# A gated MLP beside a state-space scan: Up weights in three blocks, the skip row's vector behind the B transposes, two table rows ahead of a table load, stacked half products last

## The chip, the cores and the metric

The kernel runs on one core of one Trainium2 chip. The core has a matrix engine (PE, with its weight loads shown as PEld), a vector engine (DVE), an activation engine (ACT), a general engine (POOL) and a sync engine whose queue (SP) issues most of the DMAs. The metric is device time in microseconds of one execution; less is better. The engines run side by side and meet only at semaphores.

## The reference

The input x has 2,048 tokens of 448 features. After a layer norm without weights, two branches read the normalised tokens, and their product is added to x:

```python
x = A_x
xn = _layernorm(x, axis=-1)
s = _A_ref(xn, ...)                      # diagonal complex state space, scan over the tokens
g = _silu(_B_ref(xn, B_w_gate, B_w_up, B_w_down))
return x + s * g
```

Branch A projects xn to 448 complex states by B (its real and imaginary matrices), runs `h = Lam_bar * h + Bu[t]` over all tokens, projects back by C and adds `xn * Dskip`, the skip row. Branch B is a gated MLP: `(sigmoid(xn @ w_gate) * (xn @ w_up)) @ w_down` with 1,792 hidden features. All inputs and the output are bf16.

## The kernel before

The tokens are cut into four chunks of 512 (four tiles of 128 each). For a chunk the kernel needs xn with the features on the partitions (`xnT`). Chunk 0 gets it by PE transposes, chunks 1 to 3 by DMA transposes that SP issues (`dma_transpose`, through the helper `tload`, L394).

**Gate and Up.** The 1,792 hidden features are seven steps m of 2 x 128. One step (`gu_mm`, L809 and L810) is seven pairs of matmuls with 64 contraction rows each: L809 uses partitions 0 to 63 of the weight tile and L810 partitions 64 to 127, at the same time, into the two halves of one PSUM buffer `gu` (there are three; for the fourth Gate step of chunk 0 the two `acc` banks are used). A Gate step is emptied by ACT (a tanh, L843 or L840), an Up step by DVE (L846), which multiplies the two. In chunk 0 all seven Gate steps run first, then all seven Up steps.

**Weights.** `load_w` loads one block of steps of one half (64 partitions) with one DMA on SP; the table `BLK` says which steps form a block. Gate has the blocks (0, 2), (2, 4), (4, 7), Up has (0, 3), (3, 7); each block is two DMAs, one for each half. One DMA has 64 x 7 rows of 256 bytes for each step of its block (two steps: rows of 512 bytes).

**B phase.** `b_phase` projects a chunk's xn by B into the states. B has 448 rows of features, and 448 is 3 x 128 + 64, so beside three full contraction blocks (`fulls`, L897 and L900) there is a half block (`halfrows`): L883 for the state groups 0, 1 and 2, and L886 for group 3, where the real and imaginary part are stacked on the partitions (from the tile `bT6`). Four groups of half products open or close the accumulation; the function `pairs` issues those of groups 3, 0 and 1 in this order as the first matmuls of the phase. The B matrices come by DMA transposes on SP (`b_load`): `bT` blocks 0 to 2 and block 3 of each matrix. From them POOL copies the stacked tile `bT6` (L748, L754), and DVE copies the half block of the real matrix from the upper to the lower 64 partitions (L751, key `bT3l`).

**Tables.** The scan works in a rotating frame and needs cosines and sines for 513 positions and four state groups. `scale` (L668, ACT) multiplies the positions by a group's angle, `tables` rounds on DVE (L677, L679) and takes the sines on ACT. The angle `turn` is made by POOL (L656, L658). ACT needs the silu table set for its tanh, sine and silu (`silu_table`, L664), and a set for square roots before it.

**Skip row.** `skip_row` (L545, DVE) multiplies xn by Dskip, which a DMA spreads over all partitions into the tile `dbc`.

**The order of the work.** Every operation is registered with `add` in a plan: its engine, a cost, what it reads and writes. PE's operations, and the DMAs marked `chain`, keep the order in which they are registered on their engine; so do DVE's and ACT's while `pl.seq` is true. All others are placed by a list scheduler (`solve`) by due times that follow from PE's order, from the costs, and from the times in `land`, at which a DMA is assumed to land. `HEAD_DMA` is the number of first DMAs that the scheduler numbers by registration when it models that at most eight DMAs are out at once. None of these times is a wait in the kernel: they only set the order in which each engine gets its instructions.

**The end.** `yout` makes an output tile: PE multiplies by C (L1044), DVE adds the skip row, multiplies by the gate and adds x (L1066 to L1068), SP stores it (L1057). For chunk 2 the stores of tiles 1, 2 and 3 are cut into two halves of 64 rows.

Lines of the profile that the prediction uses besides: L450 statistics of a tile of x (DVE), L540 widening copy of xn (POOL), L981 last write of the states hT of a group (DVE), L1025 the Down matmuls.

Of the kernel before, what the change touches and what calls it, by code (L numbers as in the profile page):

```python
# [18 lines left out]
D = 448  # L19
F = 1792  # L20
P = 128
H = 64
# [4 lines left out]
TPC = L // P  # L27
NTAB = L + 1
EPS = 1e-5
HEAD_DMA = 17  # L30
TWO_PI = 2.0 * math.pi
PI = math.pi
MAGIC = 12582912.0
# [213 lines left out]
def kernel(  # L247
# [18 lines left out]
    V, A, G, T, Q = nc.vector, nc.scalar, nc.gpsimd, nc.tensor, nc.sync  # L266
# [84 lines left out]
    add = pl.add  # L351
# [9 lines left out]
        load(q, [("x", t) for t in range(t0, t0 + n)], n * P * D * 2,  # L361
             x_all[:, t0:t0 + n, :], x_src[:, t0:t0 + n, :], r=r, rate=rate, land=land)

    BLK = {"g": [(0, 2), (2, 4), (4, 7)], "u": [(0, 3), (3, 7)]}

    def load_w(eng, k, half, b, r=(), rate=105e3, land=0.0):
        m0, m1 = BLK[k][b]
# [63 lines left out]
    add("POOL", 0.15, lambda: G.memset(flat(g_raw[:, 512:2048], 3, 512)[:, :, D:512], 0.0),  # L431
        w=[("xnw", t) for t in (1, 2, 3)])
    load_w("SP", "u", 0, 0, rate=400e3, land=15.6)
    load_w("SP", "u", 1, 0, rate=400e3, land=17.3)
    load_x(6, 2, land=19.3)
    load_w("SP", "u", 0, 1, rate=400e3, land=20.9)
    load_w("SP", "u", 1, 1, rate=400e3, land=22.5)
    load("SP", "dbc", P * D * 2, dbc[:], A_Dskip.unsqueeze(0).to_broadcast((P, D)), rate=400e3, land=22.7)


    def warm_mm(n, w=512):
# [224 lines left out]
    def scale(pt):  # L666
        turn, v = C("turn"), v_t[:, pt, :]
        add("ACT", 0.61, lambda: A.activation(v, iota[:, 0:NTAB], ACT.Copy, scale=turn[:, pt:pt + 1]),  # L668
            r=[("wv", 0), "turn", "silutab"], w=[("v", pt)])

    def tables():
        for pt in range(4):
            vk, nk = ("v", pt), ("nu", pt)
            v, nu = v_t[:, pt, :], nu_t[:, pt, :]
            if pt:
                scale(pt)
            add("DVE", 0.4, lambda v=v, nu=nu: V.tensor_single_scalar(out=nu, in_=v, scalar=MAGIC, op=ALU.add),  # L677
                r=[vk], w=[nk])
            add("DVE", 0.6, lambda v=v, nu=nu: V.scalar_tensor_tensor(out=nu, in0=nu, scalar=-MAGIC, in1=v,  # L679
                                                                      op0=ALU.add, op1=ALU.subtract),  # L680
                r=[vk, nk], w=[nk])
            add("ACT", 0.5, lambda v=v, nu=nu: A.activation(v, nu, ACT.Abs), r=[nk, "silutab"], w=[vk])
            so, co = (spm[:, pt, 0, :], cosT[:, pt, :]) if pt < 3 else (cs3[:, 1, :], cs3[:, 0, :])
            add("ACT", 0.537, lambda so=so, nu=nu: A.activation(so, nu[:, 0:L], ACT.Sin, scale=-S),
                r=[nk, "silutab"], w=[("sin", pt)])
            add("ACT", 0.624, lambda co=co, v=v: A.activation(co, v[:, 0:L], ACT.Sin, scale=-S, bias=pio2[:]),
                r=[vk, "silutab", "pio2"], w=[("cos", pt)])
            if pt < 3:
                add("DVE", 0.2, lambda pt=pt: V.tensor_single_scalar(out=spm[:, pt, 1, :], in_=spm[:, pt, 0, :],
                                                                     scalar=-1.0, op=ALU.mult),  # L690
                    r=[("sin", pt)], w=[("nsin", pt)])
        vs, ns = [("v", p) for p in range(4)], [("nu", p) for p in range(4)]
        cth, sth = C("cth"), C("sth")
        add("ACT", 0.2, lambda: A.activation(sinL[:, :, 0, :], nu_t[:, :, L:L + 1], ACT.Sin, scale=-S),
            r=ns + ["silutab"], w=["sinL"])
        add("ACT", 0.2, lambda: A.activation(cosL[:], v_t[:, :, L:L + 1], ACT.Sin, scale=-S, bias=pio2[:]),
            r=vs + ["silutab", "pio2"], w=["cosL"])
        add("ACT", 0.2, lambda: A.activation(sth[:].unsqueeze(2), nu_t[:, :, 1:2], ACT.Sin, scale=-S),
            r=ns + ["silutab"], w=["sth"])
        add("ACT", 0.2, lambda: A.activation(cth[:].unsqueeze(2), v_t[:, :, 1:2], ACT.Sin, scale=-S, bias=pio2[:]),  # L700
            r=vs + ["silutab", "pio2"], w=["cth"])
        add("POOL", 0.3, lambda: G.tensor_single_scalar(out=sinL[:, :, 1, :], in_=sinL[:, :, 0, :], scalar=-1.0,
                                                        op=ALU.mult), r=["sinL"], w=["nsinL"])

        gate([("vrow", q) for q in range(3)], [("hF", 0, m) for m in range(7)])
# [37 lines left out]

    def b_load():
        for i, m in enumerate((A_B_re, A_B_im)):
            tload([("bT", i)], bT[:, 0:3, i, :], m[:, 0:384], D * 768, land=24.0 + 1.4 * i)
            tload([("bT3", i)], bT[:, 3:4, i, :], m[:, 320:448], D * 256, land=24.4 + 1.8 * i)
            add("POOL", 0.7, lambda i=i: G.tensor_copy(out=bT6[:, 0:3, i * H:i * H + H], in_=bT[:, 0:3, i, 384:448]),  # L748
                r=[("bT", i)], w=[("bT6", i)])
            if i == 0:  # L750
                add("DVE", 0.3, lambda: V.tensor_copy(out=bT[0:H, 3, 0, :], in_=bT[H:P, 3, 0, :]),  # L751
                    r=[("bT3", 0)], w=["bT3l"])
            for h in range(2):
                add("POOL", 0.25, lambda i=i, h=h: G.tensor_copy(out=bT6[h * H:h * H + H, 3, i * H:i * H + H],  # L754
                                                                        in_=bT[H:P, 3, i, 384:448]),
                    r=[("bT3", i)], w=[("bT6", i, h)])
# [115 lines left out]
    def b_phase(c, mid=None):  # L872
# [14 lines left out]
                             start=start, stop=not start)  # L887

        def pairs():
            for pt in (3, 0, 1):  # L890
                halfrows(pt, True)

        def fulls(pt, first):
# [166 lines left out]
    def yout(c, j, first=False):  # L1060
        t = c * TPC + j
        g, o, q = gt_of[c, j], next_o(), t % NXD
        a = next_acc()
        key, ok, od = ("acc", a), ("o", o, 0), o_t[o][:]
        y = y_mm(c, j, acc[a], key, 0, D, False, first)
        add("DVE", dve1(D), lambda: V.tensor_tensor(out=od, in0=y, in1=xd[q][:], op=ALU.add), r=[key, ("xd", q)], w=[ok])  # L1066
        add("DVE", dve2(D), lambda: V.tensor_tensor(out=od, in0=od, in1=g_t[g][:], op=ALU.mult), r=[ok, ("gt", g)], w=[ok])
        add("DVE", dve2(D), lambda: V.tensor_tensor(out=od, in0=od, in1=x_all[:, t, :], op=ALU.add), r=[ok, ("x", t)], w=[ok])  # L1068
        rows = (0, H, P) if c == 2 and j else (0, P)
        for r0, r1 in zip(rows, rows[1:]):  # L1070
            store(t, od, 0, D, r0, r1, [ok])

# [68 lines left out]
    for t in (1, 2, 3):  # L1141
        shift(t, 1, "DVE")
        shift(t, 0, "DVE")
    gate(uk, ("gu", u2))
    silu_table()
    scale(0)
    pl.seq = False
    for t in (1, 2, 3):
        last_tile(0, "g", steps01, t, ("c", 1, "b"))
    for m in range(2):  # L1150
        gu_evac(0, "g", m, slots0[m])
    gu_mm(0, "g", 2, slots0[2], 0, TPC, False)
    gu_evac(0, "g", 2, slots0[2])
    gu_mm(0, "g", 3, None, 0, TPC, False)
    gu_evac(0, "g", 3, None)
    b_load()
    def stats_for(c):
        for t in range(4 * c, 4 * c + 4):
            if c not in (3,):
                stats(t)  # L1160
            elif t % 2:
                act_stats(t - 1)
            if t % 2:
                chain(t - 1, 2)
# [97 lines left out]
```

## Time and profile before

| what | value |
|---|---|
| median of 3 runs | 183.93 us (183.44 to 184.11) |
| the profiled execution's own time | 183.8 us |
| its span in the trace | 182.0 us |
| busy, PE | 176.8 us |
| busy, DVE | 165.9 us |
| busy, ACT | 98.1 us |
| busy, POOL | 35.1 us |
| DMA: bytes moved | 13.43 MB |
| granted clock of PE, mean | 0.997 |

How to read it: the span is the time from the first to the last recorded instruction of the profiled execution, and its own time is what the same execution was measured at; what lies between them (1.8 us) is outside the trace. Times in rows are microseconds from the span's start unless marked ns. A row of a timeline is start, duration, engine, line, operation, output <- inputs, partitions x elements, and in brackets the idle time before it with what ended it. A row of a window is the stretch, its length, and for each engine its busy time with the number of instructions; the last three numbers are PE's granted clock, the mean busy share of the 16 DMA engines and the GB/s they moved. A matmul's row shows 0.38 us for 512 columns, but the next one starts 0.21 us after it, because they are pipelined: on PE it is the starts that count.

### The profile page before, as it was taken

To read this page: it belongs to the slowest core of one execution; us is meant where nothing else is said; L and a number is where in the kernel's file an instruction comes from. 1 tells how busy PE (TensorE), PEld (TensorE's weight loads), DVE (VectorE), ACT (ScalarE), POOL (GpSimd) and SP (SyncE) were. 2 spreads that over 40 slices of the span, in tenths; PEclk is the share of its full clock that TensorE was granted. 3 is DMA by queue.
4 is the path that set the end of the run, shared out by engine and by line. 5 is a ranking of instruction groups with operands and counts; after the bars stand their busy time and mean duration, and the time that the engine had idled before them with its cause. 6 is when DMAs were issued, how large, how long until landed. Compare 5 with 4: busy or idle time off the path is not lost.

```text
span 182.0 us, 3616 instructions
## 1 busy us (share of the span) xinstructions
PE 176.8 (97%) x1404; PEld 88.1 (48%) x1411; DVE 165.9 (91%) x295; ACT 98.1 (54%) x162; POOL 35.1 (19%) x93
## 2 busy tenths in 40 slices
PE   7899999999999999999999999999999999999993
PEld 2764444564554444455554444444555444455552
DVE  2817999999989999999999999999999999999772
ACT  4899997958699994364145543348211433411101
POOL 6453537500008776000004100000000000000000
PEclk9999999999999999999999999999999999999998
DMA  5899998999300290000003900001000000001221
GB/s 137 222 203 207 201 158 171 166 342 200 105 0 0 54 151 0 0 4 0 0 2 77 142 11 0 4 0 56 20 4 0 25 27 23 6 0 62 58 65 48
DMA packets 29956, 13.43 MB, mean 74 GB/s; under 512 B 19441, under 2 KB 29938, under 8 KB 29938
## 3 DMA queue, kind: packets, MB, share of 16 engines
q1 hardware_dynamic: 29314, 12.83, 35.0%
q10 hardware_dynamic: 560, 0.36, 0.7%
q8 instruction: 11, 0.18, 0.5%
q14 instruction: 7, 0.06, 0.1%
q0 software_dynamic: 64, 0.00, 0.0%
HBM read 6.77 MB, written 1.84 MB: 47 GB/s over the span
## 4 chain that ended last, share of the span: by engine, by line
PE 85%; DMA 8%; SPq 4%; DVE 1%; issue 1%; DVEq 0%
PE gu L809 34%; PE gu L1025 15%; PE acc L1044 11%; PE acc L1025 9%; PE gu L897 8%; DMA wU<-in_B_w_up_dram 7%; PE gu L810 4%; SPq L357 4%; PE gu L883 2%; PE acc L900 2%; DMA x_all<-in_A_x_dram 1%; DVE o_t L1086 0%; PE acc L886 0%; DVE o_t L1080 0%; PE acc L1042 0%
## 5 line engine op out<-in xcount | busy, mean ns | idle before, releaser
L810 PE MATMUL gu<-xnT,wU 64*128 64x512 bf16 x196 | 46.0, 376 | 0.1
L809 PE MATMUL gu<-xnT,wU 64*128 64x512 bf16 x196 | 46.0, 376 | 0.0
L809 PE MATMUL gu<-xnT,wG 64*128 64x512 bf16 (+1 forms) x189 | 41.3, 360 | 0.0
L810 PE MATMUL gu<-xnT,wG 64*128 64x512 bf16 (+1 forms) x189 | 41.3, 360 | 0.0
L843 ACT ACTIVATE sig<-gu 128x1024 f32<-128x1024 f32 x21 | 21.3, 1020 | 25.0 <-PE gu L810 20.4
L1025 PEld LDWEIGHTS <-hF 128*128 128x128 bf16 x224 | 21.9, 98 | 20.6
L809 PEld LDWEIGHTS <-wG 64*128 64x128 bf16 x196 | 18.4, 94 | 19.9
L1025 PE MATMUL gu<-wd,hF 128*128 128x448 bf16 x140 | 28.0, 352 | 0.0
L809 PEld LDWEIGHTS <-wU 64*128 64x128 bf16 x196 | 18.3, 94 | 19.6
L846 DVE SCALAR_TENSOR_TENSOR hF<-sig,gu 128x1024 bf16<-128x1024 f32 x21 | 25.4, 1209 | 0.2
L1044 PE MATMUL acc<-cT,hT 128*128 128x448 bf16 (+2 forms) x119 | 22.9, 337 | 0.0
L964 DVE TENSOR_TENSOR_SCAN wv<-c_r,st,z 128x512 bf16<-128x512 f32 x18 | 22.9, 1276 | 0.0
L1031 ACT ACTIVATE g_t<-gu 128x448 bf16<-128x448 f32 x10 | 5.4, 540 | 27.7 <-PE gu L1025 16.8
L810 PEld LDWEIGHTS <-wU 64*128 64x128 bf16 x196 | 18.3, 94 | 3.7 <-DMA wU<-in_B_w_up_dram 0.6
L810 PEld LDWEIGHTS <-wG 64*128 64x128 bf16 x196 | 18.4, 94 | 0.0
L1025 PE MATMUL acc<-wd,hF 128*128 128x448 bf16 x84 | 16.9, 352 | 0.0
L1044 PEld LDWEIGHTS <-hT 128*128 128x128 bf16 x126 | 11.7, 98 | 9.9 <-issue 0.4
L897 PE MATMUL gu<-xnT,bT 128*128 128x512 bf16 x65 | 15.3, 379 | 0.4
L911 ACT CAST bus<-gu 128x1024 bf16<-128x1024 f32 x12 | 12.0, 1011 | 5.9 <-PE gu L883 5.3
L540 POOL COPY xn<-xn 128x448 bf16<-128x448 bf16 x12 | 8.2, 690 | 28.5 <-ACT xn L534 28.4
L450 DVE BATCH_NORM_STATS2 bst<-x_all 128x6 f32<-128x448 bf16 x11 | 6.4, 613 | 6.3 <-DMA x_all<-in_A_x_dram 6.3
L917 ACT CAST bus<-acc 64x256 bf16<-64x256 f32 (+1 forms) x24 | 8.7, 368 | 5.6 <-PE acc L900 5.3
(162 smaller groups left out, 261.7 us busy)
## 6 DMA issues: line engine op xcount, KB each, us to landing
wd<-in_B_w_down_dram SPq DMA_DIRECT2D x2, 784.0 KB, 7.4
out_dram<-o_t SPq DMA_DIRECT2D x12, 112.0 KB, 1.7
wU<-in_B_w_up_dram SPq DMA_DIRECT2D x2, 448.0 KB, 11.9
x_all<-in_A_x_dram SPq DMA_DIRECT2D x2, 448.0 KB, 5.3
wG<-in_B_w_gate_dram SPq DMA_DIRECT2D x2, 336.0 KB, 5.6
wU<-in_B_w_up_dram SPq DMA_DIRECT2D x2, 336.0 KB, 8.9
wG<-in_B_w_gate_dram SPq DMA_DIRECT2D x2, 224.0 KB, 4.5
x_all<-in_A_x_dram SPq DMA_DIRECT2D x2, 224.0 KB, 8.9
```

Source lines behind the costliest of these rows:

```text
L357: add(eng, cost, lambda: e.dma_start(out=o, in_=i), w=[key] if not isinstance(key, list) else key, r=r, dma=nbytes, chain=True, rate=rate) ...
L540: add("POOL", 0.25 if n == H else 0.6, lambda: G.tensor_copy(out=o[:, D:D + n], in_=o[:, 0:n]), r=[("xn", b)], w=[("xnw", b)])
L809: T.matmul(bank[0][:, ts], lhsT=w_[0:H, s, ms], rhs=x[0:H, SL[s], ts], start=(s == 0), stop=(s == 6))
L810: T.matmul(bank[1][:, ts], lhsT=w_[H:P, (s + 1) % 7, ms], rhs=x[H:P, SL[s], ts], start=(s == 0), stop=(s == 6))
L843: add("ACT", act(1024), lambda: A.activation(th, gu[a][:], ACT.Tanh, scale=0.5), r=[("gu", a)], w=[tk])
L846: add("DVE", dve1(1024), lambda: V.scalar_tensor_tensor(out=ho, in0=th, scalar=1.0, in1=gu[a][:], op0=ALU.add, op1=ALU.mult), r=[("gu", a) ...
L897: T.matmul(gu[slots[pt]][:, i, :], lhsT=bT[:, kt, i, pt * P:pt * P + P], rhs=x[:, kt, :], start=(first and kt == 0), stop=(not first and k ...
L911: add("ACT", act(1024), lambda: A.copy(out=bus[u][:], in_=gu[slots[pt]][:]), r=key(pt), w=[("bus", u)])
L917: add("ACT", 0.36, lambda ns=ns, d=d, q=q, l=l, i=i: A.copy(out=bus[u][d, l, ns], in_=acc[a3[i]][q, 0:256]), r=[("acc", a3[i])] + ([("bus" ...
L964: dve(1.194, lambda k=k: V.tensor_tensor_scan(out=wv[:, k, :], data0=rb, data1=z[:, k, :], initial=(st[pt][:, k, :] if c else 0.0), op0=AL ...
L1025: T.matmul(d, lhsT=hF[c % 2][:, m, h, js], rhs=wd[:, ft, :], start=(ft == 0), stop=(ft == FT - 1))
L1044: T.matmul(y, lhsT=hT[c % 2][:, hm, js], rhs=cT[:, cm, c0:c1], start=(i == 0 and not skip_on_pe), stop=(i == 6))
```

## The change

Six edits:

1. The Up weights come in blocks of 2, 2 and 3 steps in place of 3 and 4: six DMAs of 64 x 7 rows for four. The x tiles 6 and 7 stay behind the first block. The assumed landing times are adapted, and `HEAD_DMA` becomes 19.
2. The DMA of Dskip (`dbc`) moves from behind the Up weights to behind the four transposes of B. On SP it now stands right ahead of the DMA transposes of chunk 1's xn.
3. The first two rows of the sine table (`scale(0)`, `scale(1)`) are made ahead of `silu_table`, the other two behind the first two Gate evacuations, and `pl.seq` stays true that far. `scale` no longer reads the table's key, and `tables` no longer calls it.
4. The copy of the real half block (`bT3l`) goes from DVE to POOL.
5. In chunk 0, `pairs` issues the half products of the groups in the order 0, 1, 3.
6. For chunk 2 only the last tile's store is cut into halves.

```diff
-HEAD_DMA = 17
+HEAD_DMA = 19
...
-    BLK = {"g": [(0, 2), (2, 4), (4, 7)], "u": [(0, 3), (3, 7)]}
+    BLK = {"g": [(0, 2), (2, 4), (4, 7)], "u": [(0, 2), (2, 4), (4, 7)]}
...
     load_w("SP", "u", 0, 0, rate=400e3, land=15.6)
-    load_w("SP", "u", 1, 0, rate=400e3, land=17.3)
-    load_x(6, 2, land=19.3)
-    load_w("SP", "u", 0, 1, rate=400e3, land=20.9)
-    load_w("SP", "u", 1, 1, rate=400e3, land=22.5)
-    load("SP", "dbc", P * D * 2, dbc[:], A_Dskip.unsqueeze(0).to_broadcast((P, D)), rate=400e3, land=22.7)
+    load_w("SP", "u", 1, 0, rate=400e3, land=16.8)
+    load_x(6, 2, land=17.9)
+    load_w("SP", "u", 0, 1, rate=400e3, land=19.0)
+    load_w("SP", "u", 1, 1, rate=400e3, land=20.1)
+    load_w("SP", "u", 0, 2, rate=400e3, land=21.6)
+    load_w("SP", "u", 1, 2, rate=400e3, land=23.1)
...
     def scale(pt):
         turn, v = C("turn"), v_t[:, pt, :]
         add("ACT", 0.61, lambda: A.activation(v, iota[:, 0:NTAB], ACT.Copy, scale=turn[:, pt:pt + 1]),
-            r=[("wv", 0), "turn", "silutab"], w=[("v", pt)])
+            r=[("wv", 0), "turn"], w=[("v", pt)])
     def tables():
         for pt in range(4):
...
-            if pt:
-                scale(pt)
...
     def b_load():
         for i, m in enumerate((A_B_re, A_B_im)):
-            tload([("bT", i)], bT[:, 0:3, i, :], m[:, 0:384], D * 768, land=24.0 + 1.4 * i)
-            tload([("bT3", i)], bT[:, 3:4, i, :], m[:, 320:448], D * 256, land=24.4 + 1.8 * i)
+            tload([("bT", i)], bT[:, 0:3, i, :], m[:, 0:384], D * 768, land=25.0 + 1.7 * i)
+            tload([("bT3", i)], bT[:, 3:4, i, :], m[:, 320:448], D * 256, land=25.7 + 2.0 * i)
...
             if i == 0:
-                add("DVE", 0.3, lambda: V.tensor_copy(out=bT[0:H, 3, 0, :], in_=bT[H:P, 3, 0, :]),
+                add("POOL", 0.45, lambda: G.tensor_copy(out=bT[0:H, 3, 0, :], in_=bT[H:P, 3, 0, :]),
                     r=[("bT3", 0)], w=["bT3l"])
...
         def pairs():
-            for pt in (3, 0, 1):
+            for pt in (3, 0, 1) if c else (0, 1, 3):
                 halfrows(pt, True)
...
-        rows = (0, H, P) if c == 2 and j else (0, P)
+        rows = (0, H, P) if c == 2 and j == 3 else (0, P)
...
     gate(uk, ("gu", u2))
+    scale(0)
+    scale(1)
     silu_table()
-    scale(0)
-    pl.seq = False
     for t in (1, 2, 3):
         last_tile(0, "g", steps01, t, ("c", 1, "b"))
-    for m in range(2):
-        gu_evac(0, "g", m, slots0[m])
+    gu_evac(0, "g", 0, slots0[0])
+    gu_evac(0, "g", 1, slots0[1])
+    scale(2)
+    scale(3)
+    pl.seq = False
     gu_mm(0, "g", 2, slots0[2], 0, TPC, False)
     gu_evac(0, "g", 2, slots0[2])
     gu_mm(0, "g", 3, None, 0, TPC, False)
     gu_evac(0, "g", 3, None)
     b_load()
+    load("SP", "dbc", P * D * 2, dbc[:], A_Dskip.unsqueeze(0).to_broadcast((P, D)), rate=400e3, land=29.0)
+
```

## The prediction

> **What bounds the kernel now.** I read the page first: busy shares and the chain of waits.
>
> ```profile
> PE 176.8 (97%) x1404; PEld 88.1 (48%) x1411; DVE 165.9 (91%) x295; ACT 98.1 (54%) x162; POOL 35.1 (19%) x93
> ...
> PE 85%; DMA 8%; SPq 4%; DVE 1%; issue 1%; DVEq 0%
> ```
>
> A share is an average, so next I took the busy time by stage, and then the list of waits inside 15 to 36 us, which is the stretch that the change touches.
>
> ```profile
> 80.00:120.00 40.00, 39.95 (x292) 18.95 (x293) 39.96 (x64) 17.45 (x25) 2.76 (x4) 1.00 0.18 27
> ```
>
> ```profile
> PEld L810 <- DMA wU<-in_B_w_up_dram: 0.6, 1, 0.6
> PEld L886 <- POOL bT L754: 0.5, 2, 0.3
> ```
>
> In the middle stage PE and DVE both work 40 us of 40, at a granted clock of 1.00. PE sets the end: DVE's last write of hT is at 166.72, and PE reads it at 170.58, after finishing what stood ahead of it.
>
> ```profile
> 166.72 0.69 DVE L981 TENSOR_TENSOR hT<-ta,tb 128x1024 bf16<-128x1024 bf16 x1
> ```
>
> ```profile
> 170.58 0.54 PE L1044 MATMUL acc<-cT,hT 128*128 128x448 bf16 x2
> ```
>
> So DVE has 170.58 - 167.41 = 3.2 us in hand at the end, and work taken from it buys nothing by itself. PE's start and the last tile are not touched, so only the two waits of PE can be won, and they have to be priced on PE's own rows. The first is in the fourth Up step (m = 3):
>
> ```profile
> 22.28 0.38 PE L810 MATMUL gu<-xnT,wU 64*128 64x512 bf16 x1
> 22.49 0.38 PE L809 MATMUL gu<-xnT,wU 64*128 64x512 bf16 x1
> 22.95 0.39 PE L810 MATMUL gu<-xnT,wU 64*128 64x512 bf16 x1
> ```
>
> The row at 22.49 is the step's first. Pairs start every 0.21 us (22.28 to 22.49), seven pairs are a step of 1.5 us; the other half's L810 had to wait until 22.95, when the second half of the last Up block had landed. Cost: 22.95 - 22.49 - 0.21 = **0.25 us**. The second is at the head of the B phase, which I lay beside the same code one chunk later:
>
> ```profile
> 28.95 0.21 PE gu L810
> 29.16 0.09 PE acc L886
> ...
> 29.26 0.28 PE acc L886
> 29.54 0.49 PE gu L883 x4
> 30.03 0.76 PE acc L900 x6
> ```
>
> ```profile
> 39.57 0.11 PE acc L886 x2
> 39.68 0.43 PE gu L883 x4
> 40.11 0.76 PE acc L900 x6
> ```
>
> From the first half product to L900 it takes 30.03 - 29.16 = 0.87 us in chunk 0 and 40.11 - 39.57 = 0.54 in chunk 1. Cost: **0.33 us**. The most that the change can win on PE is therefore 0.25 + 0.33 = 0.58 us.
>
> **The change part by part.** The profiled execution took 183.8 us around its span of 182.0; it lies 0.1 below the median of 183.93. The sum goes against 183.8.
>
> *Up blocks.* Steps 2 and 3 now wait for the middle block alone. Are the blocks there in time?
>
> ```profile
> 14.54 0.63 DVE L450 BATCH_NORM_STATS2 bst<-x_all 128x6 f32<-128x448 bf16 x1 [2.99 <-DMA x_all<-in_A_x_dram]
> ```
>
> ```profile
> 5.00:8.00 3.00, 2.67 (x52) 2.19 (x52) 2.61 (x11) 2.49 (x10) 1.22 (x2) 1.00 0.77 194
> ...
> 18.00:20.50 2.50, 2.50 (x26) 1.13 (x24) 2.50 (x6) 2.50 (x5) 1.00 (x2) 1.00 1.12 215
> 23.00:24.50 1.50, 1.50 (x16) 0.67 (x18) 1.42 (x4) 1.50 (x3) 0.00 (x0) 1.00 1.51 53
> ```
>
> The last column is GB/s. Between 5 and 8 us the Gate weights move in runs of two steps (512 B), at 194; between 18 and 20.5 the Up weights move in runs of 1,024 B, at 215. Tiles 4 and 5 of x have landed at 14.54. Behind them come four Up transfers of 229 kB and the x pair of 229 kB: 1,147 / 194 = 5.9 us, so the middle block is whole at 20.4. PE wants it one step before 22.49, at 21.0. The last block, 688 kB at 215, takes 3.2 us more: 23.6, and step 4 wants it at 22.49 + 1.5 = 24.0. Both hold, by some 0.5 us: gain **0.25**, between 0.25 and 0. By the old rows 1,835 kB came from 14.54 to 22.95, 218 GB/s; at that rate the last block lands at 22.95 as before. I take the end of the Up weights 0.35 us later than before, between 0 and 0.65. The new order costs two more transfers on SP (0.6 us each), hidden because the queue is full then.
>
> The Trainium skill, "Perfetto Trace Analysis", DMA Optimizations, warns of small transfers and says splitting helps where the DMA engines are mostly idle. Here their share is 1.12, so by that rule the split gains nothing, and the sum would lose this 0.25; it is a rival below. The rows let me take the other side, because the first pieces are wanted sooner than the last.
>
> *Skip row's vector.* It leaves the place ahead of the B transposes: its 115 kB are 0.5 us of traffic at 215 GB/s, but part of it ran beside the Up weights' end; so between 0 and 0.5 comes free for the B matrices, and I take 0.2. The B matrices thus land 0.35 - 0.2 = 0.15 us later (between -0.5 and +0.65). DVE reads the vector for eight skip rows, which are added to output tiles far behind this stretch; the 3.2 us in hand cover a wait for it. But it now stands on SP **ahead of the four transposes of xn**:
>
> ```profile
> 26.55 5.27 SPq L394 DMA_TRANSPOSE xnT<-xn  x4
> ```
>
> ```profile
> xnT<-xn SPq DMA_TRANSPOSE x1, 3.1
> ```
>
> ```profile
> xnT<-xn SPq DMA_TRANSPOSE x1, 5.1
> ```
>
> ```profile
> 36.37 0.27 PE L809 MATMUL gu<-xnT,wG 64*128 64x256 bf16 x1
> ```
>
> SP issues the four without a pause, 1.3 us each; the second lands 3.1 us after its issue, the fourth (issued at 26.55 + 3 x 1.3 = 30.5) after 5.1: at 35.6. PE needs it at 36.37 for the second halves of chunk 1's first two steps, so there is 0.75 us of room. An issue of x costs between 0.40 and 0.77 us:
>
> ```profile
> L357 SPq DMA_DIRECT2D x_all<-in_A_x_dram x6: 403/542/765, 0.7 to 42.8; - x6
> ```
>
> I take 0.45 (a one-tile load, like the short end). What is late next: the fourth transpose, at 35.6 + 0.15 + 0.45 = 36.2.
>
> *Stacked half products last.* PE is ready for the half products at 29.16 - 0.25 = 28.91.
>
> ```profile
> 26.69 0.51 DVE L751 COPY bT<-bT 64x448 bf16<-64x448 bf16 x1
> ```
>
> ```profile
> 28.06 0.34 POOL L748 COPY bT<-bT 128x192 bf16<-128x192 bf16 x1 [0.41 <-DMA bT<-in_A_B_im_dram]
> 28.68 0.53 POOL L754 COPY bT<-bT 64x64 bf16<-64x64 bf16 x2 [0.28 <-DMA bT<-in_A_B_im_dram]
> ```
>
> The stacked products wait for the POOL copies that end at 29.21; the plain pairs wait for the last B transpose alone, which POOL took up at 28.68. So the pairs (0.43) run under the copies, and the stacked ones follow at 29.26 + 0.15 and take 0.28: L900 starts at 29.69 for 30.03. Gain of both waits together: **0.34**, between 0.58 (B not later) and 0 (B late by 0.5).
>
> *Copy of the lower rows on POOL.* DVE loses 0.51 us, hidden by its 3.2. POOL gains a copy; the nearest row is its copy of 448 columns:
>
> ```profile
> L540 POOL COPY xn<-xn x4: 555/750/1025, 18.9 to 29.3; 128x448 bf16<-128x448 bf16 x4
> ```
>
> POOL was empty for 0.41 us before 28.06 and for 0.28 before 28.68, 0.69 in all. A copy of 0.56 fits; one of 1.03 makes the last copies, and the stacked products, 0.34 late. I take nothing, since its 64 partitions and 448 columns are at most this row's work. The Trainium skill, "Perfetto Trace Analysis", Optimizing Scalar/DVE Operations, says the two engines share an SBUF read port, so that moving work between them might not help; the spread of this row agrees with that. By the rule the copy takes the long end, and the sum loses those 0.34.
>
> *Two scales ahead of the silu table.*
>
> ```profile
> 9.02 1.28 ACT L664 ACT_TABLE_LOAD   x1
> 10.44 2.86 ACT L843 ACTIVATE hF<-gu 128x1024 bf16<-128x1024 f32 x3
> 13.17 1.95 ACT L668 ACTIVATE hT<-wv,c_turn 128x513 f32<-128x513 f32 x3
> ```
>
> ```profile
> 8.77 0.23 POOL L658 TENSOR_SCALAR c_turn<-c_theta 64x1 f32<-64x1 f32 x1
> ```
>
> ```profile
> 16.45 0.38 PE L809 MATMUL gu<-xnT,wG 64*128 64x512 bf16 x1
> ```
>
> The scales' factor is ready at 9.0, when ACT comes free. ACT's total is unchanged: two scales (1.3) move ahead of 1.28 of table, then two evacuations (1.9), two scales (1.3), and the third evacuation (1.0) ends at 9.1 + 6.8 = 15.9. PE wants that bank at 16.45: covered by 0.55. If a scale needed another table load, 1.28 more would leave PE waiting 0.7. DVE gets two table rows in a stretch where it was idle (2.99 before 14.54): some lead, worth nothing on PE, as above.
>
> *The rest.* Fewer stores for two tiles near the end are off the path: the last tile's stores follow PE's last products. Due times steer a scheduler that reorders DVE, ACT and POOL; between nothing and DVE's 3.2 us in hand I take nothing.
>
> **Sum.** PE stands 0.34 earlier at the B phase and would reach the second halves at 36.03. With the fourth transpose at 36.2 it waits 0.17, and 0.17 is left; if that transpose lands 3.1 us after issue like the others, all 0.34 is left. Nearest the first: -0.2, **183.6 us**, its own range 183.3 to 183.9.
>
> **The rivals.**
>
> *Both waits vanish and nothing follows:* -0.58, 183.2. For it: the stage from 80 to 120 leaves PE 0.05 us idle, so a gain made early is kept. Against it: the traffic up to B's end is no lighter.
>
> *Slower, by the transposes of xn.* Place: the fourth transpose on SP's queue. Price: it decides from a shift of 0.7 us plus what PE has won. With the long issue (0.77), the late Up end (0.65) and one more quiet stretch like the one in the row 23 to 24.5 (53 GB/s for 1.5 us, with B waiting), the shift is 2.9 and PE starts the second halves at 38.6 for 36.37: +2.2, 186.0. Without the stretch it is 1.4: +0.7, 184.5. Middle 185.0. For it: 5.1 us of the last transpose show how easily this traffic stalls.
>
> *It doesn't do what it says:* the wait moves from step 3 to step 4 because the bytes come no sooner (688 kB at 194 end at 24.0), and B is late by as much as the reordering hides: 0, 183.8.
>
> **How the numbers follow.** Forecast 0.45, both gone 0.18, slower 0.25, no effect 0.12. 0.5% of 183.93 is 0.92 us, about what a measurement here can tell from no change: bounds 183.0 and 184.85. The PE budget of 0.58 keeps nearly every gain inside: faster 0.12 (some of the second case, by spread: the runs reach 183.44). Slower takes most of the third case and a little of the unknown order: 0.22. Same 0.66. Range 182.9 to 185.2: it holds the forecast, the best case and the slow one without its dearest end.
>
> **What would show it.** Right: the start of the fourth Up step's second pair 0.21 after its first; L900 of chunk 0 near 29.7; a wait of PE at the first L809 on 256 columns of tiles 2 and 3, or none. Wrong: gaps of PE after 40 us (from the scheduler's new order), a third table load, the bank wait at 16.45, or a middle Up block after 21.0. A gain above 0.58 would say that PE had lost time which its rows do not show.

## The result and the profile after

The change made the kernel 0.2 to 0.3% faster: 0.34 us (0.2%) by the medians, 0.27% by the ratio in the table, which is not the quotient of the two medians. The forecast counts less than 0.5% as no change. Twelve runs of each on one chip:

| what | before | after |
|---|---|---|
| median of 12 runs | 183.64 us (183.43 to 184.41) | 183.30 us (182.95 to 183.45) |
| ratio after / before, 95% interval | | 0.9973 [0.9961, 0.9985] |
| the profiled execution's own time | 183.8 us | 183.35 us |
| its span | 182.0 us | 181.5 us |

In the changed kernel the lines from the Gate blocks on have moved by one or two: L808 and L809 are the two rows of Gate and Up pairs (L809 and L810 before), L882 and L885 the plain and the stacked half products (L883 and L886), L899 the first full products (L900), L845 DVE's Up evacuation (L846). Below, "first Up" is the start of the first Up matmul of chunk 0, and "first full product" the start of L899's group (L900 before) in chunk 0, as the chain of waits has it (the chain lets a piece begin where the piece before it ends). The page of after has the same picture as that of before:

```profile
PE 177.1 (98%) x1404; PEld 88.2 (49%) x1411; DVE 166.4 (92%) x294; ACT 98.2 (54%) x162; POOL 37.6 (21%) x94
...
PE 94%; DMA 2%; SPq 1%; DVE 1%; issue 0%; DVEq 0%
```

PE sets the end in both. That its share of the chain is 94% for the 85% of before is not the change's doing: a second profile of the kernel before has 97%. The chain of waits of after, at the head of the B phase and at the last output tile (start, length, what):

```profile
28.79 0.21 PE gu L808
29.00 0.43 PE gu L882 x4
29.43 0.11 PE acc L885 x2
29.54 0.76 PE acc L899 x6
...
176.95 0.59 PE acc L1043 x7
```

The same last group in the chain of before:

```profile
177.44 0.59 PE acc L1044 x7
```

From the first full product to that group PE takes 177.44 - 30.03 = 147.41 us before and 176.95 - 29.54 = 147.41 after. So everything that the change did on PE it did ahead of 30 us, and it kept all of it. The head of the B phase now takes 29.54 - 29.00 = 0.54 us, which is what chunk 1 took before: its wait is gone. So is the other one. Rows of PE in the timeline of before, then of after, at the first and at the fourth Up step:

```profile
17.96 0.38 PE L809 MATMUL gu<-xnT,wU 64*128 64x512 bf16 x1
...
22.95 0.39 PE L809 MATMUL gu<-xnT,wU 64*128 64x512 bf16 x1
```

```profile
18.26 0.38 PE L808 MATMUL gu<-xnT,wU 64*128 64x512 bf16 x1
...
22.80 0.38 PE L808 MATMUL gu<-xnT,wU 64*128 64x512 bf16 x1
22.80 0.38 PE L809 MATMUL gu<-xnT,wU 64*128 64x512 bf16 x1
23.01 0.38 PE L808 MATMUL gu<-xnT,wU 64*128 64x512 bf16 x1
23.01 0.38 PE L809 MATMUL gu<-xnT,wU 64*128 64x512 bf16 x1
```

After, the two rows of pairs start side by side and go on at 0.21 us. From first Up to first full product it is 30.03 - 17.96 = 12.07 us before and 29.54 - 18.26 = 11.28 after: 0.79 gained. The span became only 0.5 shorter, because after's first Up came 0.30 later. That need not be the change's doing: in the fourteen profiles of this study the first Up lies anywhere from 17.70 to 18.27, with no clear order by kernel (the table below).

### The profile page after: what moved, and what is told of

Read it like the earlier page. It is cut to its first block, busy times and chain, and to the rows that moved or that the text cites. A ratio compares the mean times of both kernels' runs of the same rounds, so it can differ in the third digit from the quotient of the medians.

```text
span 181.5 us, 3611 instructions
## 1 busy us (share of the span) xinstructions
PE 177.1 (98%) x1404; PEld 88.2 (49%) x1411; DVE 166.4 (92%) x294; ACT 98.2 (54%) x162; POOL 37.6 (21%) x94
## 4 chain that ended last, share of the span: by engine, by line
PE 94%; DMA 2%; SPq 1%; DVE 1%; issue 0%; DVEq 0%
PE gu L808 43%; PE gu L1024 15%; PE acc L1043 11%; PE acc L1024 9%; PE gu L896 8%; DMA wG<-in_B_w_gate_dram 2%; PE acc L899 2%; PE gu L882 2%; SPq L357 1%; PE gu L826 1%; PE acc L808 1%; PE gu L809 1%; DVE o_t L1085 0%; PE gu L827 0%; DVE o_t L1079 0%
## 5 line engine op out<-in xcount | busy, mean ns | idle before, releaser
L808 PE MATMUL gu<-xnT,wU 64*128 64x512 bf16 x196 | 45.8, 376 | 0.0
L809 PE MATMUL gu<-xnT,wU 64*128 64x512 bf16 x196 | 45.8, 376 | 0.0
L808 PE MATMUL gu<-xnT,wG 64*128 64x512 bf16 (+1 forms) x189 | 41.3, 360 | 0.0
L809 PE MATMUL gu<-xnT,wG 64*128 64x512 bf16 (+1 forms) x189 | 41.3, 360 | 0.0
L842 ACT ACTIVATE sig<-gu 128x1024 f32<-128x1024 f32 x21 | 21.3, 1019 | 24.4 <-PE gu L809 19.8
L808 PEld LDWEIGHTS <-wU 64*128 64x128 bf16 x196 | 18.4, 94 | 22.9
L808 PEld LDWEIGHTS <-wG 64*128 64x128 bf16 x196 | 18.4, 94 | 19.9
L845 DVE SCALAR_TENSOR_TENSOR hF<-sig,gu 128x1024 bf16<-128x1024 f32 x21 | 25.4, 1210 | 0.7 <-ACT sig L842 0.4
L809 PEld LDWEIGHTS <-wU 64*128 64x128 bf16 x196 | 18.4, 94 | 0.0
L809 PEld LDWEIGHTS <-wG 64*128 64x128 bf16 x196 | 18.4, 94 | 0.0
L541 POOL COPY xn<-xn 128x448 bf16<-128x448 bf16 x12 | 7.5, 627 | 27.2 <-ACT xn L535 27.0
L535 ACT ACTIVATE xn<-x_all,nmr,rsd 128x448 bf16<-128x448 bf16 x12 | 8.8, 758 | 3.7 <-DVE xd L546 2.2
```

Of the source, the lines that this page charges most:

```text
L535: add("ACT", 0.65, lambda: A.activation(o[:, 0:448], x_all[:, t, :], ACT.Identity, bias=nmr[:, t, :], scale=rsd[:, t, :]), r=[("x", t), (" ...
L541: add("POOL", 0.25 if n == H else 0.6, lambda: G.tensor_copy(out=o[:, D:D + n], in_=o[:, 0:n]), r=[("xn", b)], w=[("xnw", b)])
L808: T.matmul(bank[0][:, ts], lhsT=w_[0:H, s, ms], rhs=x[0:H, SL[s], ts], start=(s == 0), stop=(s == 6))
L809: T.matmul(bank[1][:, ts], lhsT=w_[H:P, (s + 1) % 7, ms], rhs=x[H:P, SL[s], ts], start=(s == 0), stop=(s == 6))
L842: add("ACT", act(1024), lambda: A.activation(th, gu[a][:], ACT.Tanh, scale=0.5), r=[("gu", a)], w=[tk])
L845: add("DVE", dve1(1024), lambda: V.scalar_tensor_tensor(out=ho, in0=th, scalar=1.0, in1=gu[a][:], op0=ALU.add, op1=ALU.mult), r=[("gu", a) ...
```

## The experiments

Nine runs put one edit into the kernel before, or take one out of the changed one; three more are a pair of edits, the changed kernel again and the kernel before again. "before" in a comparison is the kernel before on the same chip in the same hours. Two accounts stood against each other. One is the forecast's: the head of the B phase waits for B's transposes and the copies made from them. The other, called D in later expectations: behind that wait stands DVE, which empties the fifth and sixth Up step too late, because it rounds table rows between two evacuations.

Since the 147.41 us are the same in all of them, each profile comes down to two stretches: first Up to first full product, and from the start of the last output group to the end of the span. All from the chain and the timeline of each run, with the end of the span taken from its trace to 0.01 us; "B" is when the last packet of B's last transpose landed.

| run | edits in it | ratio to before | first Up | first full product | between | B | end stretch |
|---|---|---|---|---|---|---|---|
| before | none | | 17.96 | 30.03 | 12.07 | 28.56 | 4.58 |
| before_again | none | 1.0003 [0.9988, 1.0019] | 18.01 | 29.49 | 11.48 | 27.93 | 4.58 |
| after | all | 0.9973 [0.9961, 0.9985] | 18.26 | 29.54 | 11.28 | 27.41 | 4.59 |
| whole_change | all | 0.9980 [0.9969, 0.9990] | 18.07 | 29.36 | 11.29 | 27.07 | 4.57 |
| one_blocks | 1 | 1.0073 [1.0060, 1.0086] | 18.23 | 30.82 | 12.59 | 27.77 | 4.95 |
| one_dbc | 2 | 0.9985 [0.9977, 0.9994] | 18.18 | 29.54 | 11.36 | 26.85 | 4.58 |
| one_scale | 3 | 0.9991 [0.9981, 1.0001] | 17.87 | 29.55 | 11.68 | 28.14 | 4.58 |
| one_stack | 5 | 1.0004 [0.9993, 1.0016] | 17.76 | 29.70 | 11.94 | 27.70 | 4.58 |
| blocks_scale | 1, 3 | 1.0008 [0.9999, 1.0018] | 18.15 | 29.43 | 11.28 | 27.59 | 4.94 |
| all_but_blocks | 2 to 6 | 0.9988 [0.9978, 0.9997] | 17.82 | 29.10 | 11.28 | 26.64 | 4.70 |
| all_but_dbc | all but 2 | 0.9989 [0.9980, 0.9997] | 18.27 | 29.65 | 11.38 | 27.47 | 4.57 |
| all_but_scale | all but 3 | 1.0044 [1.0028, 1.0060] | 17.70 | 30.27 | 12.57 | 27.91 | 4.59 |
| all_but_pool | all but 4 | 0.9975 [0.9965, 0.9985] | 18.06 | 29.34 | 11.28 | 27.15 | 4.58 |
| all_but_stack | all but 5 | 0.9981 [0.9970, 0.9991] | 17.85 | 29.13 | 11.28 | 27.32 | 4.58 |

Where "between" is 11.28, PE waits for nothing there. What stands above 11.28 is waiting.

### The Up blocks alone, and everything but them

```diff
-    BLK = {"g": [(0, 2), (2, 4), (4, 7)], "u": [(0, 3), (3, 7)]}
+    BLK = {"g": [(0, 2), (2, 4), (4, 7)], "u": [(0, 2), (2, 4), (4, 7)]}
...
+    load_w("SP", "u", 0, 2, rate=400e3, land=21.6)
+    load_w("SP", "u", 1, 2, rate=400e3, land=23.1)
```

one_blocks is before with this edit, its landing times and its `HEAD_DMA`; all_but_blocks is after without them. (The later landing times that edit 1 assumes for the B matrices stand in neither one_blocks nor blocks_scale, but they do stand in every run named all_but.)

> The kernel before with the first edit alone (Up weights in blocks of 2, 2, 3; Dskip's load stays ahead of the B transposes). Theory 1, each wait of PE belongs to its own edit: the wait in the fourth Up step goes, 0.25 us on the step's second pair and 0.2 more because the two rows of pairs were left one start apart, so the Up phase takes 10.55 us where it took 11.0; the wait at the first stacked half product stays and takes back part of it, since the B matrices come no sooner: ratio 0.9985 to 1.0. Theory 2, the smaller blocks themselves move faster and bring B about 1 us forward: the wait at the half products goes too, ratio 0.996 to 0.9975.

> The changed kernel with the Up weights in blocks of 3 and 4 again. Theory 1: PE waits 0.25 us in the fourth Up step and loses 0.2 more by the shift of the pairs, all of it kept to the end: 0.4 us over the changed kernel, ratio to the kernel before 0.999 to 1.0. Theory 2 (small blocks bring B forward): B also lands about 1 us later and the half products wait: ratio about 1.0.

one_blocks was the slowest kernel of the study: 184.66 us for 183.27. Its Up wait is gone, as expected, and B landed no later. But PE now waits at the half products, so that both expected theories missed. The wait of PE in one_blocks (us in total, times, longest), and DVE's timeline:

```profile
PE gu L885 <- DVE hF L848: 1.0, 2, 0.7
```

```profile
24.55 1.22 DVE L848 SCALAR_TENSOR_TENSOR hF<-hF,gu 128x1024 bf16<-128x1024 bf16 x1 [0.22 <-PE gu L812]
25.69 1.98 DVE L681 SCALAR_TENSOR_TENSOR hT<-hT,hT 128x513 f32<-128x513 f32 x3
27.69 0.30 DVE L753 COPY bT<-bT 64x448 bf16<-64x448 bf16 x1
28.03 3.48 DVE L848 SCALAR_TENSOR_TENSOR hF<-hF,gu 128x1024 bf16<-128x1024 bf16 x3
```

The half products need the PSUM buffers of the fifth and sixth Up step. DVE stands at 25.69, done with the fourth step; the scheduler, whose list of DMAs and assumed landing times the edit changed, has put three table roundings (1.98 us) there, so the fifth and sixth evacuations begin at 28.03 and PE waits. The kernel before has one such rounding at that place, and the same lateness in small:

```profile
25.88 0.78 DVE L679 SCALAR_TENSOR_TENSOR hT<-hT,hT 128x513 f32<-128x513 f32 x1
...
27.23 3.48 DVE L846 SCALAR_TENSOR_TENSOR hF<-hF,gu 128x1024 bf16<-128x1024 bf16 x3
```

Its sixth step is empty only at about 27.23 + 2 x 1.16 = 29.55, and the second plain pair cannot start earlier. In that profile this cost little beyond the copies: the four plain products take 0.49 us at 29.54 where they take 0.43 one chunk later. So two things held the head of the B phase in the kernel before, close behind each other, and the list of waits names only the copies. all_but_blocks (0.9988, just below the 0.999 to 1.0 that was expected) shows no wait in its one profile; old blocks do not always wait (below). Its ratio and that of the whole change, 0.9980 on another chip, have intervals that overlap, so what the blocks alone are worth in the changed kernel is not measured.

### The early scales alone, with the blocks, and everything but them

```diff
+    scale(0)
+    scale(1)
     silu_table()
-    scale(0)
-    pl.seq = False
...
+    gu_evac(0, "g", 0, slots0[0])
+    gu_evac(0, "g", 1, slots0[1])
+    scale(2)
+    scale(3)
+    pl.seq = False
```

> The changed kernel with the four table rows scaled behind the silu table again. Theory D (DVE's place in line decides): three rounding operations of the tables, 2.0 us, stand on DVE between the evacuations of the fourth and the fifth Up step, so the buffers of the fifth and sixth come free near 28.9 and 30.0; the first half products need them at 28.6 and 28.8: PE waits about 1.2 us, ratio 1.003 to 1.005. Theory P (the forecast: DVE's lead is worth nothing on PE): no wait, ratio as the whole change, 0.996 to 0.9985.

> Before with edits 1 and 3: the three Up blocks and the early scales, nothing else. Theory D (the blocks alone lost 1.35 us only because DVE then rounds three table rows between the evacuations of the fourth and the fifth Up step; with the early scales all rounding stands ahead of the first Up evacuation): no wait of PE for hF at the half products, L848's counterpart for the fifth step starts within 0.2 us of its matmuls, ratio 0.997 to 0.9995. Rival (the new blocks themselves cost, by six transfers and a later B): PE still waits at the half products, for B's copies, ratio over 1.002.

> Before with edit 3 alone. If DVE's lateness was the limit behind B's copies, PE's wait at the head of the B phase shrinks from 0.33 us to what the copies of B alone cost, 0 to 0.25, the Up wait stays as the weights land: ratio 0.9975 to 0.9995. If B's copies were the limit, as the forecast had it, the edit changes nothing: ratio 0.9995 to 1.0005, and the 0.33 us stand.

all_but_scale takes 1.0044 of before's time, inside the range of account D, with the picture of one_blocks; DVE and PE in its timeline:

```profile
25.16 2.30 DVE L680 SCALAR_TENSOR_TENSOR hT<-hT,hT 128x513 f32<-128x513 f32 x3
27.38 3.47 DVE L847 SCALAR_TENSOR_TENSOR hF<-hF,gu 128x1024 bf16<-128x1024 bf16 x3
...
29.77 0.39 PE L884 MATMUL gu<-xnT,bT 64*128 64x512 bf16 x2 [0.74 <-DVE hF L847]
```

blocks_scale has the blocks and the early scales alone, and DVE has no rounding left there:

```profile
24.40 1.22 DVE L846 SCALAR_TENSOR_TENSOR hF<-hF,gu 128x1024 bf16<-128x1024 bf16 x1
...
26.17 1.21 DVE L846 SCALAR_TENSOR_TENSOR hF<-hF,gu 128x1024 bf16<-128x1024 bf16 x1
...
27.63 1.21 DVE L846 SCALAR_TENSOR_TENSOR hF<-hF,gu 128x1024 bf16<-128x1024 bf16 x1
```

The fifth evacuation starts 1.9 us earlier than in one_blocks, "between" falls from 12.59 to 11.28, and the wait is gone: account D holds. But the ratio, 1.0008, missed the expected 0.997 to 0.9995. PE is not what lacks; its first full product comes at 29.43, and at 29.49 in before_again, run beside it. What lacks is at the end, and has its own part below. one_scale, at last, takes DVE's lateness away and leaves B as it was, and then B's copies are what PE waits for (waits of one_scale):

```profile
PEld L884 <- POOL bT L752: 0.5, 2, 0.3
...
PEld L808 <- DMA wU<-in_B_w_up_dram: 0.2, 1, 0.2
```

So both limits are real, one behind the other. Of the 0.40 us that it waits in all (11.68 - 11.28) the longest wait for the copies is 0.3. Its ratio of 0.9991 lies in D's range, and its interval reaches into the other one.

### The skip row's vector alone, and everything but it

```diff
-    load("SP", "dbc", P * D * 2, dbc[:], A_Dskip.unsqueeze(0).to_broadcast((P, D)), rate=400e3, land=22.7)
...
     b_load()
+    load("SP", "dbc", P * D * 2, dbc[:], A_Dskip.unsqueeze(0).to_broadcast((P, D)), rate=400e3, land=29.0)
```

> The kernel before with the second edit alone (Dskip's load behind the B transposes, ahead of the xn transposes). Theory 1: the Up wait of 0.25 stays; the B matrices land 0.2 to 0.5 us earlier, and so does the first stacked product: ratio 0.998 to 0.9995. Theory 3, Dskip's load (one row of HBM read 128 times) is what held the B transposes back: B lands about 1 us earlier, the wait of 0.33 at the half products goes, ratio 0.9975 to 0.9985. If its place ahead of the xn transposes costs anything, the first L809 on tiles 2 and 3 of chunk 1 waits: ratio above 1.

> After without edit 2: the skip row's vector stands ahead of the B transposes again. If moving it brings B forward by 0.9 us, B's last transpose lands at 27.9 to 28.6 and its last copy on POOL ends at 28.6 to 29.4, so the stacked products at 29.2 to 29.5 wait for 0 to 0.2 us: ratio to before 0.998 to 0.9995. If the move is worth nothing by itself (the earlier B of the other runs was chance), B lands at 27.1 to 27.9 and the ratio is 0.997 to 0.9985 as for the whole change.

one_dbc alone brings 0.9985, more than half of what the whole change brings by the ratios. That is the common end of both expected ranges; that B landed about 1 us earlier speaks for theory 3, and PE does not wait at the first L809 on tiles 2 and 3. With the old blocks, B landed at 26.85 and 26.64 with the vector moved, and at 27.70, 27.93, 28.14 and 28.56 without. With the new blocks the difference fades: 27.07 to 27.91 with it moved (five profiles), 27.47, 27.59 and 27.77 without. all_but_dbc agrees: B landed at 27.47, earlier than expected, and of the stretch "between" only 0.10 is lost. The ratio fell into the range expected if the move brings B forward, B's landing into that of the other account. And the 0.10 does not come from B, whose copies are done at 28.11. With the vector there early, DVE makes a skip row ahead of its evacuation of the fifth Up step, and the sixth is empty only at 29.10 (in after at 28.92). DVE's timeline of all_but_dbc:

```profile
25.66 0.38 DVE L547 TENSOR_TENSOR xd<-g_t,dbc 128x448 bf16<-128x448 bf16 x1
...
27.89 1.21 DVE L846 SCALAR_TENSOR_TENSOR hF<-hF,gu 128x1024 bf16<-128x1024 bf16 x1
```

So in the changed kernel this edit is worth about 0.1 us in that profile, by DVE's order and not by B; by the ratios, from two chips and with intervals that overlap, it is not clear of noise.

### Stacked half products last, alone and left out

```diff
-            for pt in (3, 0, 1):
+            for pt in (3, 0, 1) if c else (0, 1, 3):
```

> The kernel before with the order of the half products alone (stacked ones last in chunk 0). Theory 1: the pairs run under the POOL copies, PE starts L900 0.3 to 0.45 us earlier, ratio 0.9978 to 0.999. Rival: the pairs wait for the last B transpose just as the stacked products wait for the copies, 0.1 us is won, ratio 0.9990 to 1.0005.

> The changed kernel with the stacked half products first again; only PE's order differs. Theory 1 (the reordering hides the POOL copies): PE waits 0.3 us for them, ratio 0.998 to 0.9995. Theory D: the copies end before PE arrives (28.2 against 28.8 in the first profile), so nothing is lost, and stacked ones first even leave DVE 0.1 us more for the buffers: ratio as the whole change, 0.996 to 0.9985.

Neither differs from its counterpart. Alone, the pairs start early and run into DVE (PE and DVE in the timeline of one_stack):

```profile
26.80 3.48 DVE L846 SCALAR_TENSOR_TENSOR hF<-hF,gu 128x1024 bf16<-128x1024 bf16 x3
...
29.20 0.39 PE L883 MATMUL gu<-xnT,bT 64*128 64x512 bf16 x2 [0.32 <-DVE hF L846]
```

That is the ratio that the rival expected, but not for its reason: the second pair waits for DVE and not for B. The order had been hiding DVE's wait behind that for the copies. In the changed kernel the last of B's copies are done before PE gets there, so the order does not matter: 0.9981 without it, 0.9980 with it.

### The copy back on DVE

```diff
-                add("POOL", 0.45, lambda: G.tensor_copy(out=bT[0:H, 3, 0, :], in_=bT[H:P, 3, 0, :]),
+                add("DVE", 0.3, lambda: V.tensor_copy(out=bT[0:H, 3, 0, :], in_=bT[H:P, 3, 0, :]),
```

> The changed kernel with the copy of B's lower rows on DVE. It stands between the evacuations of the fifth and the sixth Up step. Theory D: 0.3 to 0.5 us of DVE, plus a wait for B's transpose where that lands late, push the sixth step's evacuation past the second half product: PE loses 0.1 to 0.5 us, ratio 0.998 to 1.0. Theory P: nothing, 0.996 to 0.9985.

0.9975, with no wait in the profile: the move to POOL is worth nothing either way. The copy did not stand where the expectation had it, though: DVE made it at 25.77, ahead of the fifth evacuation at 26.07. POOL's copies in after:

```profile
25.76 0.56 POOL L750 COPY bT<-bT 64x448 bf16<-64x448 bf16 x1
...
27.52 0.66 POOL L753 COPY bT<-bT 64x64 bf16<-64x64 bf16 x2
```

They end at 28.18, and the half products stand in PE's chain at 29.00.

### The changed kernel again and the kernel before again

> The changed kernel as it is, once more, as the yardstick for the three beside it. Ratio 0.996 to 0.9985 as before. If the 0.31 us that PE waited for a Gate transfer near 7 us in the first profile belong to the change, they come again; if they vary from run to run, they need not.

> The kernel before once more, unchanged. It shows how far two profiles of the same kernel lie apart: if the two waits are steady, 0.25 us at the fourth Up step and 0.33 us at the head of the B phase again, each within 0.1, and B's last transpose lands at 28.6 within 0.3; if the transfers vary from run to run, the Up wait lies anywhere from 0 to 0.4 and B lands at 27.5 to 29. Ratio 0.9993 to 1.0007 either way.

whole_change repeats the gain on another chip: 183.05 us for 183.27. The 0.31 us that PE waited for a Gate transfer near 7 us in the first profile did not come again. before_again says how far one profile can be trusted. Its waits, in the same stretch as the two rows that the forecast was built on:

```profile
PEld L883 <- issue: 0.7, 2, 0.4
PEld L900 <- issue: 0.2, 1, 0.2
PEld L886 <- POOL bT L754: 0.2, 1, 0.2
```

No wait for the Up weights, and 0.20 us of waiting in all (11.48 - 11.28) where the first profile had 0.79. In the six profiles with the old blocks a wait for the Up weights shows in three (before, one_stack, one_scale); in the eight with the new blocks in none. The forecast's profile, 183.8 us, was of an execution slower than the median of its own twelve (183.64); on the chips of the three later comparisons the kernel before had medians of 183.27, 183.27 and 183.32. How much of that lies in the chip is not separated.

### The end of the kernel

No run was made for this; it was found in the profiles above. blocks_scale and one_blocks end 0.4 us later behind their last output group than the others. SP's last wait, in before, after, blocks_scale, one_blocks and all_but_blocks, one fence each:

```profile
SPq L1257 <- DMA out_dram<-o_t: 0.8, 1, 0.8
```

```profile
SPq L1261 <- DMA out_dram<-o_t: 0.8, 1, 0.8
```

```profile
SPq L1260 <- DMA out_dram<-o_t: 1.2, 1, 1.2
```

```profile
SPq L1259 <- DMA out_dram<-o_t: 1.2, 1, 1.2
```

```profile
SPq L1259 <- DMA out_dram<-o_t: 1.0, 2, 0.7
```

The last line of the program waits for all DMAs. The kernel's DMAs report on eight counters in turn (no view of the profile prints them; the traces hold them): the last store reports on the eighth counter in before and after, on the second in blocks_scale and one_blocks, on the sixth in all_but_blocks. Edit 1 adds two DMAs, and so moves the last store two counters on; edit 6 takes two stores away and moves it back. That fits the end stretch of all fourteen: 4.57 to 4.59 where the last store is on the eighth, 4.94 and 4.95 on the second, 4.70 on the sixth. The traces also show how. SP takes its waits on the counters one after another, 0.06 us apart where nothing holds them. In before the last store's counter is the last one that SP waits for. In blocks_scale it is the first: that store landed at 180.50, and six more waits followed, the last at 180.88. In all_but_blocks two followed. From the landing of the last store to the end of the span it took 0.92 us in before, 1.04 in all_but_blocks and 1.28 in blocks_scale.

all_but_dbc and blocks_scale, run beside each other, differ by edits 4, 5 and 6, of which 4 and 5 were worth nothing, and by the assumed landing times: 183.16 for 183.53 us, while PE's first full product was no earlier. So edit 6 is worth about 0.4 us beside edit 1. Edit 6 was not run by itself; without edit 1 it would put the last store on the sixth counter, as in all_but_blocks.

## Why the prediction was right, and where its steps were not

**The forecast** was 183.6 us with a range of 182.9 to 185.2, and no measurable difference as the likeliest. The median came out at 183.30, 0.34 us below before. What bounds the kernel was right: PE carried the end, and what could be won stood in two waits ahead of 30 us. Of the cases it was the second that happened on PE, both waits gone with nothing behind them (183.2). The budget was wrong: 0.79 us were won in the profile where 0.58 was said to be the most, and the rows had shown it.

**Up blocks, 0.25.** The wait went, but it was mis-sized. I took off one start of 0.21 us from 22.95 - 22.49, as if the rows of pairs took turns. The rows of after at the fourth step show that they start side by side. In before L810 starts 0.46 late, at 22.95 beside the second L809, and stays one start behind (28.95 in the chain). The wait's price was the whole 0.46. With the 0.33 at the B phase that makes the 0.79. Against this, such a wait shows in half the profiles with the old blocks.

**The landing of the Up weights and of B.** I priced transfers in 512 B runs at 194 GB/s from the stretch 5 to 8 us. That was a slow stretch of that execution: in the same window before_again moved 227. After, the windows of 5 to 8, 18 to 20.5 and 23 to 24.5 us (GB/s last):

```profile
5.00:8.00 3.00, 2.79 (x49) 2.06 (x49) 2.50 (x11) 2.30 (x8) 1.28 (x2) 1.00 0.91 222
18.00:20.50 2.50, 2.50 (x26) 1.15 (x24) 1.44 (x6) 2.50 (x5) 0.94 (x2) 1.00 1.59 226
23.00:24.50 1.50, 1.50 (x16) 0.68 (x14) 1.22 (x1) 1.50 (x4) 0.77 (x2) 1.00 0.83 161
```

The same 512 B runs moved at 222, and smaller runs were not slower. The Trainium skill ("Perfetto Trace Analysis", DMA Optimizations) says that splitting may let some chunks start sooner, and gives as the case for it that the DMA engines are mostly idle. I weighed the second half alone, by which the split should have gained nothing at a share above 1. The traces agree with the first half: the split did not make the bytes faster, and in eight profiles with it the fourth step does not wait for Up weights, where three of six without it do. By the times alone the blocks' gain is not clear of noise.

**Skip row's vector, and the transposes of xn.** I had B 0.15 us later; it landed 1.15 earlier than in the profile of before (27.41 for 28.56), but only 0.52 earlier than in the second profile of before (27.93). With the vector moved it came at 26.64 to 27.91 in seven profiles, without at 27.47 to 28.56 in seven: earlier on the whole, with an overlap. The rival in which the fourth transpose of xn comes late did not happen. SP's queue in the timeline of after and PE where the fourth is wanted, then the fourth transpose's time from issue to landing:

```profile
24.69 0.58 SPq L357 DMA_DIRECT2D dbc<-in_A_Dskip_dram  x1
25.39 5.28 SPq L394 DMA_TRANSPOSE xnT<-xn  x4
...
35.88 0.27 PE L808 MATMUL gu<-xnT,wG 64*128 64x256 bf16 x1
```

```profile
xnT<-xn SPq DMA_TRANSPOSE x1, 3.0
```

The vector's issue cost 0.58, between the forecast's ends of 0.40 and 0.77, but B's issues had ended earlier, so the four began 1.16 us sooner than before (25.39 for 26.55). The fourth landed at 25.39 + 3 x 1.34 + 3.0 = 32.4: 3.5 us of room, where I had 0.17 us of waiting.

**Stacked half products last, 0.34 for both waits.** The step is refuted. I took the row "PEld L886 <- POOL" for the whole reason of the 0.33. The second plain pair could not start before DVE's 29.55, and in one_stack L900 comes 0.50 behind that pair (29.70 for 29.20). By these rows, as an estimate, the new order alone would have brought L900 to 30.05, where it was 30.03. It gains nothing alone (1.0004), and in the changed kernel it is not needed.

**Copy on POOL.** Right: 0.56 us, as the short end of the nearest row said. By the rule of the Trainium skill on the two engines' shared port ("Perfetto Trace Analysis", Optimizing Scalar/DVE Operations), as I read it, it would have cost 0.34; the run with the copy on DVE and that with it on POOL do not differ (0.9975 and 0.9980). Rightly nothing.

**Two scales ahead of the table: "some lead, worth nothing on PE".** This is the step that failed. The work is as forecast, except that the third evacuation came ahead of the last two scales; ACT in after:

```profile
9.19 1.35 ACT L669 ACTIVATE hT<-wv,c_turn 128x513 f32<-128x513 f32 x2
10.56 1.28 ACT L665 ACT_TABLE_LOAD   x1
11.85 2.86 ACT L842 ACTIVATE hF<-gu 128x1024 bf16<-128x1024 f32 x3
14.58 1.34 ACT L669 ACTIVATE hT<-wv,c_turn 128x513 f32<-128x513 f32 x2
```

One table load, and the third evacuation done at 14.7, well ahead of the 16.45 at which PE wants the bank. But DVE's lead is worth 1.2 us on PE in the changed kernel (184.22 for 183.05). I had argued from DVE's 3.2 us in hand at the end of the kernel. That slack says nothing of 25 to 29 us, where DVE empties the buffers that PE's next matmuls need; the row of three evacuations in one piece, 27.23 to 30.7, stood in the trace of before.

**Order by the scheduler: taken as nothing.** Wrong in the same way. In one_blocks the scheduler put 2 us of roundings on that spot, and the kernel lost 0.7%, of which about 0.2 is the end stretch. The landing times were not changed without the blocks.

**Fewer stores: "off the path".** True of the stores themselves, and wrong of the end: beside two more loads they are worth 0.4 us, as the end stretches above show.

**The sum.** -0.2 was forecast. The profile gave 0.79 on PE less 0.30 at the head, and the medians -0.34 and -0.22 on two chips. The errors went against each other: a wait worth more than priced, in a profile that waited more than the next one of the same kernel, and three edits that I had at nothing, of which one (the scales) keeps the change from losing 1.2 and one (the stores) from losing 0.4. That the number came out near was in part luck: without the scales, which the sum had at nothing, the same change is slower than before.

## What to carry to other kernels

Slack at the end of an engine's work is no licence for one of its stretches: where PE waits for copies, look also at when the buffers of its next matmuls are emptied, because the list of waits named only one of the two here. Before a budget is read from waits of one profile, look at how far a second profile of the same kernel agrees; here 0.79 us became 0.20. And count the DMAs: a change that adds or removes two can move the end of the kernel by tenths, through the place that the last store's counter has among SP's last waits.

## What was not expected of the hardware

Data traffic falls nearly silent for about a microsecond while DMA transposes are under way, and in each of the six profiles looked at (before, before_again, after, all_but_dbc, one_dbc, one_scale) a 16 KB fetch on the instruction queue stood at the beginning of it or ahead of it. The DMA view of before_again from 22.3 to 24.6 us in 40 slices, with that queue:

```profile
GB/s 285 285 303 557 272 272 276 229 272 263 272 249 31 18 0 0 0 0 0 0 9 4 9 9 9 9 13 4 9 9 9 13 9 9 9 102 272 289 238 214
...
q8 instruction: 1, 0.02, 2.7%
```

From 260 GB/s it falls to under 20 for 1.3 us and comes back. The fetch is not needed for such a lull: in all_but_blocks, with transposes under way, traffic lies at 26 GB/s or less from 20.5 to 21.3 us, and the first fetch on that queue after 18 us comes at 21.87. What causes the lulls, and whether a fetch deepens them, stays open.
